# Batches 1 to 7 of attention + SwiGLU: from a planned order to an order written out over ten streams

## The chip, the cores and the metric

The kernel runs on one core of a Trainium2 chip. The metric is device time in microseconds (us), as the median of the runs shown. Five engines work side by side, each through its own queue in order: TensorE (PE in the profile; its weight loads are PEld), VectorE (DVE), ScalarE (ACT), GpSimd (POOL) and SyncE (SP), which issues the DMAs.

## The reference

Two blocks follow each other. First, an attention between the tokens of a sequence and a small set of states, in both directions, for 8 batches and 8 heads (`x` is 8 x 8 x 512 x 64, `state` 8 x 8 x 32 x 64):

```python
scores = scale * np.matmul(x, state.transpose(0, 1, 3, 2))
a = softmax(scores)                     # over the 32 states
xread = np.matmul(a, state)
scores2 = scale * np.matmul(state, x.transpose(0, 1, 3, 2))
a2 = softmax(scores2)                   # over the 512 tokens
sread = np.matmul(a2, x)
attn_out = np.concatenate([xread, sread], axis=2)
```

The result, 8 x (512 + 32) rows of 512 (heads side by side), goes through an RMS norm and a SwiGLU feed-forward with a hidden width of 1536:

```python
xn = x / sqrt(mean(x * x) + 1e-6) * rms_g
g = xn @ w_gate
silu = g * (1.0 / (1.0 + np.exp(-g)))
val = xn @ w_val
out = silu * val @ w_out
```

All is float32; the three weights arrive in float64 and are converted on the chip.

## The kernel before, in words

**Stages.** Weights are converted while batch 0 is computed. Then come batches 1 to 7 (512 token rows each), and last one stage for the 256 state rows of all batches.

**Own weights.** The token read of a batch is a product of softmax weights and 32 states, so the kernel does not form `xn`. It multiplies the states into gate and val weights first (`own_weights`, L430: 16 matmuls on quarters of the array at L437, two copies by ACT to `v` at L446), and the hidden product is then softmax weights times `v`. The raw weights lie in DRAM in six parts `w_m`; `fetch` loads part n + 3 into the buffer that part n leaves (three buffers).

**Products by sevens.** In batches 1 to 7 a product of 2 x 2 blocks is done with seven block products instead of eight. POOL forms the sums of blocks: `slot_sums` (L505) of the softmax weights, four instructions a batch, and `more_of_v` (L457) of `v`, four a pair. `hidden_seven(b, mp)` (L514) does one pair of hidden tiles out of six: seven products of four matmul instructions (L522), into three PSUM banks x, y, z (pool `fx` has two banks, `fy` and `fz` one each). ACT copies x, z, x out (L532, L534, L539), DVE adds y, z, x (L537, L541, L543), ACT does tanh (L547), DVE makes silu x val (L548, L552). From the fourth pair on DVE also makes sums for the projection (L557, L559). `project_seven` (L616) is the projection by `w_out`: seven products of 24 matmul instructions (L626), each in two row halves r, over banks x, y, z again; ACT keeps four results (L646), DVE adds three (L651) and updates the block sums `s` twice (L659, L668); each half of a result is stored by a DMA on SP.

**Attention inside.** In the loop over batches (L743) the attention of batch b + 1 runs beside the products of batch b: `tokens_read` (L251: transposes, scores at L275, softmax on DVE and ACT, the reads at L320, sums of squares at L334, the norm at L344) and `states_read` (L348). `some(n)` advances it by n steps at given places. POOL's `pow` at L238 makes the inverse root.

**What sets the order.** In batch 0 a string, `ORDER` (L22), deals out single steps of fourteen streams under `tc.manual_schedule` (L726), and PE, DVE and ACT keep that order. From batch 1 on nothing is fixed: a planner orders each engine's instructions by what it takes to be ready, by its own costs; the order of the program is only a priority. POOL and SP are the planner's throughout. An instruction that waits holds back all behind it on its engine.

Of the kernel before, what the change touches and what calls it, by code (L numbers as in the profile page):

```python
# [26 lines left out]
    "AhwpuSSSkkkwSwkpSkpwpSSckSScckkpcSwkkk"  # L27
# [4 lines left out]
def kernel(  # L32
# [364 lines left out]
    def attention(b):  # L397

        if 2 < b + 1 < B:
            load_state(b + 1)  # L400
            load_x(b + 1)
        for part in (tokens_read(b), states_read(b)):
            for step in part:
                if step:
                    yield

    def state_norm():

        sq = one.tile([P, NI, NT], F32, name="sqT", tag="eS")
        SE.activation(out=sq, in_=xsT, func=ACTF.Square, scale=DM ** -0.5)  # L410
        sp = aps.tile([P, NT // P], F32, name="at")
        for r in range(NT // P):
            for i in range(NI):
                TE.matmul(out=sp[:, r:r + 1], lhsT=sq[:, i, P * r:P * r + P], rhs=ones,
                          start=(i == 0), stop=(i == NI - 1))
        ss = two.tile([P, NT // P], F32, name="sst")
        VE.tensor_scalar(ss, sp, 1e-6, None, op0=ALU.add)
        rp = along_rows(mean_root(ss, NT // P), NT // P)
# [11 lines left out]
    def own_weights(b, mp):  # L430

        w = w_sb.pop(b * (NM // 2) + mp)
        pv = [vps.tile([P, 4 * P], F32, name="pv") if b else
              aps.tile([P, 4 * P], F32, name="at") for e in range(2)]
        for j in range(4):
            for e in range(2):
                TE.matmul(out=pv[e][Ns * j:Ns * j + Ns, :],  # L437
                          lhsT=stT_g[b][D * e:D * e + D, j, :],
                          rhs=w[D * e:D * e + D, j].rearrange("p m k f -> p (m k f)"),
                          start=True, stop=True)  # L440
# [10 lines left out]
        yield  # L451

    def make_v(b, mp):
        for _ in own_weights(b, mp):
            pass
# [58 lines left out]
    def hidden_seven(b, mp):  # L514

        v, vs = v_sb.pop((b, mp))
        tt = aT_t[b]
        b11, t3, b21, b22 = (aT_s[b][:, e, HS * i:HS * i + HS] for e in range(2) for i in range(2))
# [6 lines left out]
        a11, a12, s3, a22 = (v[:, e, :, k, :] for k in range(2) for e in range(2))  # L525
        g = two.tile([P, 2, 2, HS], F32, name="g", tag="g")
        c22 = seven["c22"].tile([P, 2, HS], F32, name="c22")
        xs = fx.tile([P, 2, HS], F32, name="f")
        ys = fy.tile([P, 2, HS], F32, name="f")
        zs = fz.tile([P, 2, HS], F32, name="f")  # L530
        product(xs, a11, b11, True)
        SE.copy(g[:, :, 0, :], xs)  # L532
        product(zs, vs[:, 0], tt[:, 0], True)
        SE.copy(c22, zs)  # L534
        yield
        product(ys, a12, b21, True)
        VE.tensor_tensor(out=g[:, :, 0, :], in0=g[:, :, 0, :], in1=ys, op=ALU.add)  # L537
        product(xs, vs[:, 1], tt[:, 1], False)
        SE.copy(g[:, :, 1, :], xs)  # L539
        product(zs, vs[:, 2], b22, False)  # L540
        VE.tensor_tensor(out=g[:, :, 1, :], in0=g[:, :, 1, :], in1=zs, op=ALU.add)  # L541
        product(xs, s3, t3, False)
        VE.tensor_tensor(out=c22, in0=c22, in1=xs, op=ALU.add)  # L543
        yield
        h = hb[:, 2 * mp:2 * mp + 2, :]
        gate = g.rearrange("p m c t -> p m (c t)")
        SE.activation(out=h, in_=gate, func=ACTF.Tanh, scale=0.5)  # L547
        VE.scalar_tensor_tensor(out=h, in0=h, scalar=1.0, in1=gate, op0=ALU.add, op1=ALU.mult)  # L548
        product(xs, a22, tt[:, 2], False)
        for i, val in enumerate((xs, c22)):  # L550
            half = h[:, :, HS * i:HS * i + HS]
            VE.scalar_tensor_tensor(out=half, in0=half, scalar=0.5, in1=val,  # L552
                                    op0=ALU.mult, op1=ALU.mult)
        if 2 * mp >= HM:
            k = 2 * mp - HM
            upper, lower = (hb[:, k:k + 2, HS * i:HS * i + HS] for i in range(2))
            VE.tensor_tensor(out=seven["s"][:, k:k + 2, :], in0=lower, in1=h[:, :, HS:S],  # L557
                             op=ALU.add)
            VE.tensor_tensor(out=lower, in0=upper, in1=lower, op=ALU.subtract)  # L559
        yield  # L560
# [37 lines left out]
    def prepare(b):  # L598
        if b < B:
            slot_sums(b)  # L600
            make_v(b, 0)

# [13 lines left out]
    def project_seven(n, store, between, prepare):  # L616
# [4 lines left out]
        def product(ps, lhs, rhs, start):  # L621


            for r in range(R):
                for k in range(HM):
                    TE.matmul(out=ps[:, r, :], lhsT=lhs(k)[:, P * r:P * r + P], rhs=rhs(k),  # L626
                              start=(start and r == 0 and k == 0),
                              stop=(k == HM - 1), skip_group_check=True)

# [12 lines left out]
        def keep(ps):  # L642

            kept = [pool.tile([P, HD], F32, name="ot2") for r in range(R)]
            for r in range(R):
                SE.copy(kept[r], ps[:, r, :])  # L646
            return kept

        def finish(kept, ps, i, j):
            for r in range(R):  # L650
                VE.tensor_tensor(out=kept[r], in0=kept[r], in1=ps[:, r, :], op=ALU.add)  # L651
                store(R * i + r, HD * j, HD, kept[r])

        zs = fz.tile([P, 2, HD], F32, name="f")
        product(zs, S_, TS(0), True)
        p5 = keep(zs)
        for r in range(R):
            c = slice(P * r, P * r + P)
            VE.tensor_tensor(out=s[:, :, c], in0=s[:, :, c], in1=hb[:, 0:HM, c], op=ALU.subtract)  # L659
        xs = fx.tile([P, 2, HD], F32, name="f")  # L660
        product(xs, A(0, 0), B(0, 0), True)
        p1 = keep(xs)
        between()
        product(xs, S_, TS(1), False)
        u2 = keep(xs)
        for r in range(R):
            c = slice(P * r, P * r + P)
            VE.tensor_tensor(out=s[:, :, c], in0=hb[:, HM:NM, c], in1=s[:, :, c], op=ALU.subtract)  # L668
        between()
        product(xs, A(1, 0), B(0, 1), False)  # L670
        finish(p5, xs, 1, 1)
        ys = fy.tile([P, 2, HD], F32, name="f")
        product(ys, A(0, 1), B(1, 0), True)
        finish(p1, ys, 0, 0)
        between()
        prepare()
        product(zs, S_, B(1, 1), False)
        finish(u2, zs, 0, 1)
        product(xs, A(1, 1), TS(2), False)
        for r, c21 in enumerate(keep(xs)):  # L680
            store(R + r, 0, HD, c21)
        between()
# [22 lines left out]
    def first_of_batch_1():  # L705
        slot_sums(1)
        yield
        yield from own_weights(1, 0)
        yield
# [6 lines left out]
    for k in range(1, RAW_AHEAD):  # L716
# [8 lines left out]
               "w": first_of_batch_1(), "k": weight_sums()}  # L725
    with tc.manual_schedule(engines={mybir.EngineType.PE, mybir.EngineType.DVE,  # L726
                                     mybir.EngineType.Activation}):
# [5 lines left out]
    for stream in streams.values():  # L733
        for _ in stream:
            pass
# [3 lines left out]
    def some(n):  # L739
        for _ in range(n):  # L740
            next(steps, done)

    for b in range(1, B):  # L743
        steps = attention(b + 1) if b + 1 < B else state_norm()
        pairs = [hidden_seven(b, mp) for mp in range(NM // 2)]
        next(pairs[0])
        for mp, pair in enumerate(pairs):
            if mp + 1 < len(pairs):
                make_v(b, mp + 1)
            next(pair)  # L750
            if mp + 1 < len(pairs):
                next(pairs[mp + 1])
            next(pair)
            some(2)
        project_seven(S, store_tokens(b), lambda: some(5), lambda: prepare(b + 1))
        for _ in steps:
            pass
# [8 lines left out]
    project_seven(NT, store_states, lambda: None, lambda: None)  # L766
# [30 lines left out]
```

## Time and profile before

| | |
|---|---|
| median of 3 runs | 843.95 us (843.67 to 845.07) |
| the profiled execution | 844.68 us, its span 842.9 us |
| granted TensorE clock, mean | 0.984 |
| busy: PE, PEld | 811.1 us (96%), 591.4 us (70%) |
| busy: DVE, ACT, POOL | 474.3 us (56%), 341.4 us (41%), 164.5 us (20%) |
| the chain that ended last | PE 82%, DVE 14%, issue 2%, ACT 1% |
| one of batches 2 to 6 | 92.86 us |

The span goes from the first instruction to the last. A row of the chain of waits has start, length and what was at work ("PE f L626 x18": 18 matmuls into tile f by line 626). A row of the groups has busy time and the mean of one instruction in ns, then the idle time before them and what ended it. A row of the timeline has start and length in us; idle time and its releaser stand in brackets. A row of windows has, for a stretch, its length, then busy time and count of PE, PEld, DVE, ACT and POOL, the granted clock, the share of the DMA engines and GB/s.

### The profile page before, as it was taken

Reading aid. Unit: us, or ns where it says so; the run is one execution under the profiler, and the core shown is the slowest. Engines: PE = TensorE matmul, PEld = TensorE weight load, DVE = VectorE, ACT = ScalarE, POOL = GpSimd, SP = SyncE. Lnnn points to the kernel's source line nnn. Section 1 sums busy time; section 2 is a strip of 40 time slices with the busy share of each in tenths; the row PEclk is TensorE's granted clock in tenths of the full one; section 3 lists DMA queues with packets and bytes.
Section 4 is the critical chain, followed back from the end, with each engine's and each line's share of the span. In section 5 each row is a group of like instructions: output and inputs, shape, how many; then the busy total and the mean of one; then the engine's idle time right before and its main releaser. Section 6 shows DMA issues by size and latency. Waiting matters only on the chain.

```text
span 842.9 us, 11794 instructions
## 1 busy us (share of the span) xinstructions
PE 811.1 (96%) x4678; PEld 591.4 (70%) x4678; DVE 474.3 (56%) x750; ACT 341.4 (41%) x560; POOL 164.5 (20%) x215
## 2 busy tenths in 40 slices
PE   4699999999999999999999999999999999999997
PEld 3243445768876787768776787668776887788886
DVE  5989986695148723693169614792169515651121
ACT  5888755552055313642155304631255304510110
POOL 0000004231134012421143112311223113400000
PEclk8599999999999999999999999999999999999999
DMA  9788736222233033312342043310322023401211
GB/s 293 240 275 291 259 152 200 104 98 54 88 123 140 4 78 128 145 54 51 101 150 101 4 125 125 105 46 13 138 101 100 2 87 113 150 1 38 113 50 26
DMA packets 61591, 94.09 MB, mean 112 GB/s; under 512 B 38752, under 2 KB 46432, under 8 KB 54624
## 3 DMA queue, kind: packets, MB, share of 16 engines
q1 hardware_dynamic: 59456, 92.81, 32.7%
q8 instruction: 37, 0.61, 0.3%
q10 hardware_dynamic: 2080, 0.52, 0.3%
q14 instruction: 18, 0.15, 0.1%
HBM read 78.12 MB, written 15.20 MB: 111 GB/s over the span
## 4 chain that ended last, share of the span: by engine, by line
PE 82%; DVE 14%; issue 2%; ACT 1%; DMA 0%; SPq 0%; POOL 0%; DVEq 0%
PE f L626 33%; PE f L522 24%; PE f L480 5%; PE f L569 4%; PE pv L437 4%; PE pv L480 4%; PE at L266 2%; DVE g L541 1%; DVE g L537 1%; DVE eS L297 1%; PE at L275 1%; PE at L334 1%; DVE c L543 1%; DVE hb L552 1%; DVE hb L548 1%
## 5 line engine op out<-in xcount | busy, mean ns | idle before, releaser
L522 PE MATMUL f<-aT_s,v 128*128 128x256 f32 x504 | 130.9, 393 | 0.0
L522 PEld LDWEIGHTS f<-aT_s,v 128*128 128x128 f32 x504 | 89.3, 189 | 48.0 <-issue 28.5
L626 PE MATMUL f<-wo,hb 128*128 128x256 f32 x540 | 121.5, 380 | 0.0
L626 PEld LDWEIGHTS f<-wo,hb 128*128 128x128 f32 x540 | 102.0, 190 | 15.5 <-ACT ot L646 1.9
L464 POOL TENSOR_TENSOR vs<-v 128x256 f32<-128x256 f32 x42 | 33.2, 791 | 304.4 <-ACT v L446 304.4
L522 PE MATMUL f<-aT_t,vs 128*128 128x256 f32 x336 | 86.7, 380 | 1.9 <-DVE g L541 1.9
L626 PE MATMUL f<-wt,hs 128*128 128x256 f32 x360 | 86.9, 387 | 0.0
L646 ACT COPY ot<-f 128x256 f32<-128x256 f32 x60 | 19.6, 375 | 163.2 <-PE f L626 163.2
L446 ACT COPY v<-pv 128x512 f32<-128x512 f32 x84 | 46.0, 591 | 92.2 <-PE pv L437 92.2
L626 PEld LDWEIGHTS f<-wt,hs 128*128 128x128 f32 x360 | 65.7, 190 | 15.0 <-issue 4.9
L651 DVE TENSOR_TENSOR ot<-ot,f 128x256 f32<-128x256 f32 x45 | 17.2, 418 | 104.4 <-PE f L626 54.8
L522 PEld LDWEIGHTS f<-aT_t,vs 128*128 128x128 f32 x336 | 63.3, 190 | 13.0 <-POOL v L466 4.2
L537 DVE TENSOR_TENSOR g<-g,f 128x512 f32<-128x512 f32 x42 | 28.6, 680 | 75.0 <-PE f L522 72.8
L547 ACT ACTIVATE hb<-g 128x1024 f32<-128x1024 f32 x42 | 44.4, 1056 | 42.3 <-DVE g L541 42.3
L548 DVE SCALAR_TENSOR_TENSOR hb<-hb,g 128x1024 f32<-128x1024 f32 x42 | 51.4, 1224 | 8.2 <-ACT hb L547 8.2
L437 PE MATMUL pv<-w_m,stT_g 64*32 64x512 f32 x672 | 52.9, 600 | 0.0
L238 POOL TENSOR_TENSOR ri<-ss,mhalf 128x4 f32<-128x4 f32 x8 | 9.1, 1142 | 207.3 <-DVE ss L338 113.4
L522 PE MATMUL f<-aT_t,v 128*128 128x256 f32 x168 | 43.8, 383 | 4.0 <-DVE c L543 4.0
L480 PE MATMUL pv<-aT_s,v 128*128 128x512 f32 x96 | 46.4, 624 | 1.1 <-DVE aT_s L344 1.1
L569 PE MATMUL f<-wo,hb 128*128 128x512 f32 x96 | 44.7, 600 | 0.0
L522 PE MATMUL f<-aT_s,vs 128*128 128x256 f32 x168 | 43.1, 379 | 0.0
L541 DVE TENSOR_TENSOR g<-g,f 128x512 f32<-128x512 f32 x42 | 28.7, 682 | 23.9 <-PE f L522 23.9
(117 smaller groups left out, 1261.9 us busy)
## 6 DMA issues: line engine op xcount, KB each, us to landing
w_m<-w_d SPq DMA_DIRECT2D x48, 1024.0 KB, 4.8
x_b<-in_x_dram SPq DMA_DIRECT2D x30, 256.0 KB, 4.8
out_dram<-ot SPq DMA_DIRECT2D x56, 128.0 KB, 1.8
raw<-in_moe_w_val_dram SPq DMA_DIRECT2D x6, 1024.0 KB, 5.2
raw<-in_moe_w_out_dram SPq DMA_DIRECT2D x6, 1024.0 KB, 7.1
w_d<-w_m SPq DMA_DIRECT2D x6, 1024.0 KB, 4.9
raw<-in_moe_w_gate_dram SPq DMA_DIRECT2D x5, 1024.0 KB, 5.5
raw<-in_moe_w_gate_dram SPq DMA_DIRECT2D x2, 512.0 KB, 4.5
```

The source lines that it names most:

```text
L437: TE.matmul(out=pv[e][Ns * j:Ns * j + Ns, :], lhsT=stT_g[b][D * e:D * e + D, j, :], rhs=w[D * e:D * e + D, j].rearrange("p m k f -> p (m k ...
L446: SE.copy(v[:, e].rearrange("p m k f -> p (m k f)"), pv[e])
L464: GE.tensor_tensor(out=vs[:, 0], in0=a21, in1=a22, op=ALU.add)
L480: TE.matmul(out=to[0][:, 0:n], lhsT=lhs(i, k), rhs=r, start=(i == 0), stop=(i == len(rhs) - 1))
L522: TE.matmul(out=ps[:, i, :], lhsT=lhs[:, i, :], rhs=rhs, start=(start and i == 0), stop=True, skip_group_check=True)
L537: VE.tensor_tensor(out=g[:, :, 0, :], in0=g[:, :, 0, :], in1=ys, op=ALU.add)
L541: VE.tensor_tensor(out=g[:, :, 1, :], in0=g[:, :, 1, :], in1=zs, op=ALU.add)
L547: SE.activation(out=h, in_=gate, func=ACTF.Tanh, scale=0.5)
L548: VE.scalar_tensor_tensor(out=h, in0=h, scalar=1.0, in1=gate, op0=ALU.add, op1=ALU.mult)
L569: TE.matmul(out=banks[r], lhsT=hb[:, m, P * r:P * r + P], rhs=wo[:, m, :], start=(m == 0), stop=(m == NM - 1))
L626: TE.matmul(out=ps[:, r, :], lhsT=lhs(k)[:, P * r:P * r + P], rhs=rhs(k), start=(start and r == 0 and k == 0), stop=(k == HM - 1), skip_gr ...
L646: SE.copy(kept[r], ps[:, r, :])
```

## The change

Batches 1 to 7 get an order for PE, DVE and ACT as batch 0 has one. A new string `PERIOD` deals out the steps of one batch over ten streams: h, t, u (hidden products, ACT's part, DVE's part), p, c, k (the projection's), v (own weights of pairs 2 to 5), a and s (the next batch's attention) and w (the next batch's `slot_sums` and own weights of pairs 0 and 1). The same string serves every batch; letters without a stream are passed over in batch 7, where a is the norm of the states, one step in seven.

`hidden_seven` becomes three generators with a new sequence of products. Within pair m: x by the second sum of weights, z by the third, y, x by s3, then the first two products of pair m + 1 (x by a11, z by the first sum), then the last product of pair m. The first row half of the projection's first product stands before the last product of pair 5. The projection begins with x = A00 B00 and comes to z (by sums), y, x (by sums), x = A10 B01, z = S B11, x = A11 T; before it began with z by sums, and y was fifth. Copies and sums out of a bank are dealt by row halves; the copy of u2's first half comes between the halves of the product by sums into x, and the copy of its second half between the halves of the next. `own_weights` makes four steps (matmuls, two copies, POOL's sums), and own weights of two pairs are made ahead: those of batch 1's pair 1 move into the end of batch 0 (four more letters w in `ORDER`). The state stage calls the same projection in a sequence of 16 steps, and is otherwise as before.

The diff, cut to its core:

```diff
+PERIOD = (
+    "hhtvthhthhuhuuhtuuhthatavhuvtaavauhahauahvtutaauhuhtvvuahhaahthvsuvuhhatatuutuhv"
+    "hvtvshushuhsuhtvhuthtvauhuuuuhvhtsuhuussshtsvhsthauushatutuhhuhpuuuhtsuuupsuapau"
+    "aaakcpkcacsppaaakaaapaccpapakaakcaaaaaapaawkwwwpwkwpkppwkwcwck"
 )
...
         for e in range(2):
             SE.copy(v[:, e].rearrange("p m k f -> p (m k f)"), pv[e])
-            if e == 0:
-                yield
-        if b in aT_t:
+            yield
+        if b:
             more_of_v(b, mp)
-        yield
+            yield
...
+            yield from first(0, pairs[0])
+            for mp, q in enumerate(pairs):
+                if mp:
+                    last(pairs[mp - 1])
+                    yield
+                product(q["x"], q["vs"][:, 1], tt[:, 1], False)
+                yield
+                product(q["z"], q["vs"][:, 2], b22, False)
+                yield
+                q["y"] = fy.tile([P, 2, HS], F32, name="f")
+                product(q["y"], q["a12"], b21, True)
+                yield
+                product(q["x"], q["s3"], t3, False)
+                yield
+                if mp + 1 < len(pairs):
+                    yield from first(mp + 1, pairs[mp + 1])
+            last(pairs[-1])
+            yield
...
+        def sums():
+            for mp, q in enumerate(pairs):
+                h = hb[:, 2 * mp:2 * mp + 2, :]
+                g = q["g"]
+                for to, ps in ((g[:, :, 1, :], "z"), (g[:, :, 0, :], "y"), (q["c"], "x")):
+                    VE.tensor_tensor(out=to, in0=to, in1=q[ps], op=ALU.add)
+                    yield
...
+        def products():
+            yield from product("x", A(0, 0), B(0, 0))
+            yield from product("z", S_, TS(0))
+            yield from product("y", A(0, 1), B(1, 0))
+            yield from product("x", S_, TS(1))
+            yield from product("x", A(1, 0), B(0, 1))
+            yield from product("z", S_, B(1, 1))
+            yield from product("x", A(1, 1), TS(2))
+
+        def copies():
+
+            for what, name in (("p1", "x"), ("p5", "z"), ("u2", "x"), ("c21", "x")):
+                for r in range(R):
+                    to = kept[what, r] = pool.tile([P, HD], F32, name="ot2")
+                    SE.copy(to, banks[name][:, r, :])
...
+        def sums():
+            yield from less(s, s, hb[:, 0:HM])
+            yield from add("p1", "y", 0, 0)
+            yield from less(s, hb[:, HM:NM], s)
+            yield from add("p5", "x", 1, 1)
+            yield from add("u2", "z", 0, 1)
...
     for b in range(1, B):
-        steps = attention(b + 1) if b + 1 < B else state_norm()
-        pairs = [hidden_seven(b, mp) for mp in range(NM // 2)]
...
-        project_seven(S, store_tokens(b), lambda: some(5), lambda: prepare(b + 1))
...
+        if b + 2 < B:
+            load_state(b + 2)
+            load_x(b + 2)
+        h, t, u = hidden_seven(b)
+        p, c, k = project_seven(S, store_tokens(b))
...
+        streams = {"h": h, "t": t, "u": u, "p": p, "c": c, "k": k,
+                   "v": (step for mp in range(2, NM // 2) for step in own_weights(b, mp))}
+        if b + 1 < B:
+            streams.update(a=tokens_read(b + 1), s=states_read(b + 1), w=first_of_batch(b + 1))
+        else:
+            others = paced(state_norm())
+            streams["a"] = others
+        with tc.manual_schedule(**by_hand):
+            for stream in PERIOD:
+                if stream in streams:
+                    next(streams[stream])
...
-    project_seven(NT, store_states, lambda: None, lambda: None)
+    p, c, k = project_seven(NT, store_states)
+    for step in (p, c, p, c, k, p, k, p, c, k, p, k, p, k, p, c):
+        next(step)
```

More of the change, by code (lines that the diff above doesn't have):

```diff
@@ L512, in slot_sums, with hidden_seven @@
         GE.tensor_tensor(out=b12, in0=b22, in1=b12, op=ALU.subtract)
[L514 to L518, printed above, removed]
+    def hidden_seven(b):
+        pairs = [{} for mp in range(NM // 2)]
         def product(ps, lhs, rhs, start):
@@ L523, in product @@
                           stop=True, skip_group_check=True)
[L525 to L559, printed above, removed]
@@ L562, in project_as_ready @@
+        return products(), copies(), sums()
     def project_as_ready(banks):
@@ L655, in project_seven @@
[L655 to L682, printed above, removed]
+        kept = {}
+        def products():
+            yield from product("x", A(0, 0), B(0, 0))
[5 more added lines that the diff above has]
+            yield from product("x", A(1, 1), TS(2))
```

146 lines of the change are left out of this document (93 added, 53 removed).

## The prediction

> **What bounds the kernel now.** I read the busy table first, then the chain of waits, then the windows by batch, and the timeline of TensorE where the chain leaves it.
>
> ```profile
> span 842.9 us, 11794 instructions
> PE 811.1 (96%) x4678; PEld 591.4 (70%) x4678; DVE 474.3 (56%) x750; ACT 341.4 (41%) x560; POOL 164.5 (20%) x215
> ...
> PE 82%; DVE 14%; issue 2%; ACT 1%; DMA 0%; SPq 0%; POOL 0%; DVEq 0%
> ```
>
> TensorE sets the end; no transfer does. But its busy time is made of overlapping records, so 96% doesn't say how much is left. The pitch of the starts does:
>
> ```profile
> 779.09 41.44 PE f L480 x192
> 820.52 18.14 PE f L626 x84
> ...
> 838.69 0.37 ACT ot L646
> ```
>
> At the end of the kernel 192 matmuls of 256 columns take 41.44 us, 0.2158 us each (18.14 / 84 agrees), with no wait among them. That is my unit. Now one batch, number 2, from its first product to that of batch 3 (the chain inside a window, which cuts the last row):
>
> ```profile
> 231.95 1.73 PE f L522 x8
> 233.68 1.02 PE pv L437 x16
> 234.70 6.32 PE f L522 x28
> ...
> 241.13 0.44 PE at L266 x4
> ...
> 287.11 0.79 PE at L334 x8
> ...
> 324.81 1.29 PE f L522 x6
> ```
>
> A batch takes 324.81 - 231.95 = 92.86 us. It has six pairs of 28 product matmuls (gate and val, L522) and 168 of projection (L626): 336 x 0.2158 = 72.5 us. The remaining 20.4 us are the other matmuls, and what is lost between them. The chain leaves TensorE for DVE and ACT from about 259 to 282 us, where the next batch's softmax runs beside pairs 4 to 6. The windows of batch 2, of batch 7, and of the stretch of batch 0 that already has its order by hand:
>
> ```profile
> 231.95:324.81 92.86, 91.68 (x567) 69.94 (x567) 50.24 (x83) 34.54 (x62) 23.16 (x29) 1.00 0.28 92
> ...
> 696.26:779.09 82.83, 82.77 (x435) 65.69 (x435) 39.06 (x57) 24.87 (x42) 14.87 (x21) 1.00 0.21 77
> ...
> 80.00:135.40 55.40, 55.40 (x211) 23.58 (x210) 51.98 (x68) 38.44 (x49) 7.62 (x9) 1.00 0.56 196
> ```
>
> The last row is the best witness for this change: where PE, DVE and ACT each follow a written order, TensorE has no idle time in 55.4 us although DVE is busy for 51.98 of them.
>
> **The change, part by part.** It removes no arithmetic in batches 1 to 7: the same matmuls, copies and sums are issued. What can be gained is lost time alone, so I price a batch without it and compare with 92.86.
>
> (a) The reads of the next batch (L320). Now the planner puts them out as their inputs come, and TensorE waits inside them; in the hand-ordered stretch the same 16 matmuls stand together:
>
> ```profile
> 370.81 1.82 PE L320 MATMUL at<-aT_s,rows 32*64 32x512 f32 x6
> ...
> 373.75 1.13 PE L522 MATMUL f<-aT_t,v 128*128 128x256 f32 x4 [0.67 <-DVE c L543]
> 374.82 1.07 PE L320 MATMUL pv<-aT_s,rows 32*64 32x512 f32 x2
> 375.81 0.91 PE L626 MATMUL f<-wt,hs 128*128 128x256 f32 x3
> ```
> ```profile
> 98.01 0.66 PE L320 MATMUL at<-aT_s,rows 32*64 32x512 f32 x4
> ...
> 99.05 3.70 PE L569 MATMUL f<-wo,hb 128*128 128x512 f32 x8
> ```
>
> From 370.81 to 373.75 and from 374.82 to 375.81 are 3.93 us; together they are 1.04. Gain 2.9, and 0.2 for one change of array shape less. The new list puts them behind y (both halves, 5.2 us) and the first half of x by the sums (2.6), 7.8 us after the first product of sums ends. The last softmax steps on DVE are late there, since in its list they stand behind the addition of y:
>
> ```profile
> L651 DVE TENSOR_TENSOR ot<-ot,f 128x256 f32<-128x256 f32 x45 | 17.2, 418 | 104.4 <-PE f L626 54.8 <-issue 49.6
> ...
> L313 DVE STREAM_TRANSPOSE aT_s<-eS 128x512 f32<-128x512 f32 x16 | 11.3, 704 | 0.1
> ```
>
> 5.2 + 0.42 + some 0.55 for the reciprocal + two of 0.7, and five hand-overs of 0.05 to 0.25, make 8.1: I charge 0.3.
>
> (b) Waits for a PSUM bank inside a pair. The product by s3 goes into the bank that ACT has just copied, with one product between; the new sequence has two between each write, copy and next write:
>
> ```profile
> 345.62 0.59 ACT L539 COPY g<-f 128x512 f32<-128x512 f32 x1 [0.74 <-PE f L522]
> ...
> 346.26 1.38 PEld L522 LDWEIGHTS f<-aT_s,v 128*128 128x128 f32 x7 [0.21 <-ACT g L539]
> ```
> ```profile
> 363.10 1.97 PE L522 MATMUL f<-aT_s,v 128*128 128x256 f32 x8
> 365.39 1.10 PE L522 MATMUL f<-aT_t,vs 128*128 128x256 f32 x4 [0.32 <-DVE g L541]
> ```
>
> The weight load is 0.21 late, and costs the matmul stream 0.08 (28 products take 6.32 instead of 6.04, 0.28 more, of which the change of shape around L437 is 0.2). Six times: 0.5. The second fence is a bank that waits for DVE: 365.39 - 363.10 = 2.29 for eight matmuls (1.73), 0.56 once a batch. With two products between (8 x 0.2158 = 1.73) a copy of 0.59 or a sum of 0.68 and its hand-overs fit. Gain 1.05. What waits next is the sum of val (L543), with two products of cover as well.
>
> (c) The split group of own weights with the scores, and the state reads, now and in the hand-ordered stretch:
>
> ```profile
> 350.35 1.04 PE L437 MATMUL pv<-w_m,stT_g 64*32 64x512 f32 x2
> ...
> 352.97 1.13 PE L522 MATMUL f<-aT_s,v 128*128 128x256 f32 x4
> ```
> ```profile
> 389.57 1.40 PE L381 MATMUL at<-x_b,e2T 128*32 128x64 f32 x64
> 390.90 1.13 PE L626 MATMUL f<-wt,hs 128*128 128x256 f32 x4
> ```
> ```profile
> 135.96 1.10 PE L381 MATMUL at<-x_b,e2T 128*32 128x64 f32 x64
> 136.99 1.13 PE L522 MATMUL f<-aT_s,v 128*128 128x256 f32 x4
> 137.96 0.27 PE L392 MATMUL at<-ident,sr 128*128 128x128 f32 x1
> 138.07 1.88 PE L569 MATMUL f<-wo,hb 128*128 128x512 f32 x4
> ```
>
> 2.62 for two groups of 1.02 and 0.2 for the shapes: 0.4 gained; 1.33 against 1.03: 0.3.
>
> The new batch from the bottom: 72.5 of products; six groups of own weights at 1.02 + 0.2 = 7.3; scores 1.2; reads 1.23 + 0.3; state reads 1.2; sums of squares (0.79 above) 0.9; 30 transposes at 0.11 = 3.3. Sum 87.9, a gain of **4.96 a batch**. From the top, (a) to (c) name 3.1 - 0.3 + 1.05 + 0.7 = 4.55; the other 0.4 are slips of 0.1 in the projection, which I don't trace. Bounds: the sum without the 0.3 and with perfect switches is 87.0; from the other side, at least (a) alone goes, 90.0.
>
> (d) The seam of batches 0 and 1. The fence above shows the first product of batch 1 (136.99) put between L381 and L392 while DVE scales the reads; two lists one after the other can't do that, so 0.95 is lost. One group of own weights (1.22) moves ahead to here. Now from 136.99 to 231.95 are 94.96; then: 0.95 + 0.11 + 1.72 of batch 0's last matmuls + 1.22 + 87.9 = 91.9. Gain 3.06.
>
> (e) Batch 7 has 82.83 now. Its new list: 72.5 + four groups 4.9 + state norm 2.2, and a new loss.
>
> ```profile
> 705.16 1.84 PE L414 MATMUL at<-ones,sqT 128*128 128x1 f32 x16
> 706.94 1.05 PE L437 MATMUL pv<-w_m,stT_g 64*32 64x512 f32 x4
> ```
>
> State norm is 706.94 - 705.16 and two transposes. The copy of u2's first half stands between the two halves of the product into that same bank, and again one product later; in batches 1 to 6 the reads and the sums of squares lie between, in batch 7 nothing. Price: a copy of 0.37 (the last row of the second fence), and on either side of it a hand-over of some 0.2, an estimate: in (b) the weight load starts 0.05 behind the copy's end (345.62 + 0.59 to 346.26) and itself takes time. That is 0.8, twice, 1.6. Sum 81.2, gain 1.6; if halves of a bank don't wait for each other, 3.2.
>
> [...]
>
> (f) At nothing: the state stage (the same 276 matmuls; no wait is seen in them now, and the new order keeps a product of 2.6 us behind each sum); fetches of weights, still three groups ahead, the tightest some 20 us; the loads of x, one batch ahead on SP's queue as now. POOL's four sums of weights for a pair start when the pair two before it has left their buffer:
>
> ```profile
> L467 POOL TENSOR_TENSOR vs<-v,vs 128x256 f32<-128x256 f32 x42 | 37.3, 888 | 0.0
> ```
>
> Four of at most 0.89 make 3.5 us beside a pair of about 8; without that cover each of the four pairs would wait some 2 us.
>
> **Sum.** 3.06 + 5 x 4.96 + 1.6 = 29.5 us. The profiled execution took 844.68 (span 842.9 and 1.8 around it), 0.73 above the median of the three runs, 843.95. So 844.68 - 29.5 = 815.2 on its scale, and 843.95 - 29.5 = **814.5** for the median.
>
> **The rivals.**
>
> 1. *The waits come back.* A list stalls at its head, where the planner slipped something else in. In the profile's favour: DVE's list is full around the hand-over to projection. Against it: the row of 80 to 135 us. If two thirds of what (a) to (c) win return (3 us a batch), 814.5 + 6 x 3 = 832; a third gives 823. Chance 0.16.
>
> 2. *Only TensorE's idle time can go.* The batch window has 92.86 - 91.68 = 1.18 idle, batch 7 0.06: 6 x 1.18 = 7, so 837. Against it: a record of 0.38 in a pitch of 0.2158 covers a slip of 0.1 wholly. Chance 0.04. [...]
>
> 3. *DVE becomes the bound, and it gets slower.* The projection's second product needs all six pairs' sums. Ahead of it DVE has:
>
> ```profile
> L548 DVE SCALAR_TENSOR_TENSOR hb<-hb,g 128x1024 f32<-128x1024 f32 x42 | 51.4, 1224 | 8.2 <-ACT hb L547 8.2
> ...
> L541 DVE TENSOR_TENSOR g<-g,f 128x512 f32<-128x512 f32 x42 | 28.7, 682 | 23.9 <-PE f L522 23.9
> ```
>
> A pair is five instructions of 0.68 and one of 1.22, 4.6 us; the last three pairs have two more each: 32 us, and 5 of attention. TensorE's list up to there is 36.2 (42 products) + 4.9 (own weights) + 2.4 (scores, state reads) + 2.8 (25 transposes) + 5.2 (first product) = 51.5 us, of which DVE can use 46, since its first sum waits for five products and a group. So it is late only if its rows grow by a quarter; from 40% on the loss (37 x 1.4 - 46 = 5.8) eats the 4.96. At 50%, 9.5 a batch: 814.5 + 6 x 9.5 = 872. These rows don't vary with their neighbours now. Chance 0.04; with other losses over 5 us a batch, 0.06 for slower.
>
> 4. *The order isn't kept, or buffers undo it:* the time stays at 844. The order of batch 0 is kept in the trace, but for what follows it. Chance 0.03.
>
> **How the numbers follow.** The forecast (809 to 820) has 0.69, rival 1 0.16, rival 2 0.04, no change 0.03, slower 0.06; 0.02 stay below 809. The range holds the forecast and the milder two thirds of rival 1: 808 (every batch at 87.0, no loss in (e)) to 829. About 0.2% (1.7 us) is what a measurement of this kernel can tell from no change. Faster 0.91, same 0.03, slower 0.06.
>
> **What would show it.** Right: a batch of about 88 us from x of pair 0 to the next; L320 in one block of 16; no weight load waiting for L539's copy; two gaps of 0.7 in batch 7's projection. Wrong: TensorE waiting for DVE at the projection's second product or at L320 (rivals 1, 3), for POOL at the product by the first sum of weights (f), or for a fetch at L437.

## The result, and the profile after

The changed kernel takes **811.83 us** (median of four runs, 811.29 to 812.39) against 844.51 for the kernel before, measured beside it (843.67 to 845.18): a ratio of 0.9614, with a 95% interval from 0.9597 to 0.963. The forecast was 814.5. The profiled execution took 811.35, its span is 809.6. Times below are medians too; one execution of the planned order that took 2690.84 us is left out.

The head of the page of the changed kernel, with the busy time of each engine and the chain of waits by engine:

```profile
span 809.6 us, 11777 instructions
PE 785.6 (97%) x4678; PEld 589.2 (73%) x4678; DVE 483.5 (60%) x750; ACT 337.5 (42%) x560; POOL 156.4 (19%) x215
...
PE 94%; DVE 4%; ACT 1%; issue 0%; DMA 0%; SPq 0%; DVEq 0%
```

The same 4678 matmuls now end 33 us sooner, yet PE's share of the span goes only from 96% to 97%: busy time fell with the span, because it had held the lost time. DVE's part of the chain falls from 14% to 4%. The chain inside a window, batch 2 of the changed kernel, from its first product to that of batch 3:

```profile
227.42 1.73 PE f L517 x8
...
302.27 1.02 PE pv L438 x16
303.29 2.79 PE f L665 x12
...
315.06 1.08 PE f L517 x5
```

A batch is 315.06 - 227.42 = 87.64 us, where it was 92.86, and no row of the window's chain is on another engine than PE. The windows of this batch, of batch 7 and of the state stage up to the start of its last matmul, then two rows of TensorE's waits, summed over the kernel (us in total, times, longest):

```profile
227.42:315.06 87.64, 87.64 (x567) 69.49 (x567) 51.76 (x83) 34.03 (x62) 21.75 (x29) 1.00 0.31 97
665.63:746.75 81.12, 81.12 (x427) 67.70 (x427) 39.34 (x57) 25.74 (x43) 12.35 (x17) 1.00 0.19 65
746.75:804.94 58.19, 57.73 (x267) 50.49 (x267) 11.74 (x29) 5.99 (x16) 0.00 (x0) 1.00 0.19 65
```
```profile
PE at L375 <- ACT e L368: 5.6, 1, 5.6
...
PE f L665 <- ACT ot L698: 0.5, 1, 0.5
```

Everything in that list but the wait at L665 lies ahead of batch 1. The waits of before for the sums (L522 for c L543 and g L541, 4.0 and 1.9 us in all) are gone. Where the 33.3 us of the two profiled spans come from, by the start of the first product matmul of each stage:

| stage | before | after | change | forecast |
|---|---|---|---|---|
| up to batch 1's first product | 136.99 | 136.24 | -0.75 | 0 |
| batch 1 with the seam behind batch 0 | 94.80 | 91.02 | -3.78 | -3.06 |
| batches 2 to 6, each | 92.86 | 87.64 | -5.22 | -4.96 |
| batch 7 and the state stage, to the last matmul | 142.18 | 139.47 | -2.71 | -1.6 |

0.75 + 3.78 + 5 x 5.22 + 2.71 = 33.34. The first row isn't the change's: the kernels below start batch 1 between 135.7 and 137.3 without a cause in their edits (one that moves this product itself apart). In batches 2 to 6 some 2 us are left above the pitch of 0.2155 to 0.2158 us a matmul, counted from the starts of the matmuls (some 7 before; how much exactly depends on what an undisturbed group of small matmuls is taken to cost). They stand at the changes of array shape alone, some 0.09 ahead of a group of small matmuls, 0.09 inside it and 0.10 behind.

The timeline of TensorE where the next batch's state is read, and in batch 7's projection:

```profile
289.17 2.75 PE L665 MATMUL f<-wt,hs 128*128 128x256 f32 x12
291.86 0.66 PE L326 MATMUL at<-aT_s,rows 32*64 32x512 f32 x4
291.88 0.66 PE L326 MATMUL pv<-aT_s,rows 32*64 32x512 f32 x4
292.34 0.61 PE L326 MATMUL at<-aT_s,rows 32*64 32x512 f32 x4
292.36 0.61 PE L326 MATMUL pv<-aT_s,rows 32*64 32x512 f32 x4
292.90 2.86 PE L665 MATMUL f<-wt,hs 128*128 128x256 f32 x12
```
```profile
726.73 1.03 PE L476 MATMUL f<-xsT,w_m 128*128 128x256 f32 x4
727.59 2.75 PE L665 MATMUL f<-wt,hs 128*128 128x256 f32 x12
730.18 2.75 PE L665 MATMUL f<-wo,hb 128*128 128x256 f32 x12
732.77 1.03 PE L476 MATMUL f<-xsT,w_m 128*128 128x256 f32 x4
...
794.07 2.75 PE L665 MATMUL f<-wt,hs 128*128 128x256 f32 x12
797.28 2.86 PE L665 MATMUL f<-wo,hb 128*128 128x256 f32 x12 [0.46 <-ACT ot L698]
```

The reads are one block of 16, 291.86 to 292.90. In batch 7 the planner put eight matmuls of the state stage (L476) into the two places where I had forecast waits. In the state stage itself, where nothing is left to put in, the same wait stands at 797.28.

### The profile page after: what moved, and what is told of

It is laid out like the page before. It is cut to its first block, busy times and chain, and to the rows that moved or that the text cites. A ratio compares the mean times of both kernels' runs of the same rounds, so it can differ in the third digit from the quotient of the medians.

```text
span 809.6 us, 11777 instructions
## 1 busy us (share of the span) xinstructions
PE 785.6 (97%) x4678; PEld 589.2 (73%) x4678; DVE 483.5 (60%) x750; ACT 337.5 (42%) x560; POOL 156.4 (19%) x215
## 4 chain that ended last, share of the span: by engine, by line
PE 94%; DVE 4%; ACT 1%; issue 0%; DMA 0%; SPq 0%; DVEq 0%
PE f L665 34%; PE f L517 32%; PE pv L438 5%; PE f L476 5%; PE f L607 5%; PE pv L476 4%; PE at L272 2%; PE at L326 1%; PE at L281 1%; PE at L340 1%; PE at L387 1%; PE at L438 1%; PE at L375 1%; DVE ex L222 1%; DVE raw L218 1%; PE at L251 1%
## 5 line engine op out<-in xcount | busy, mean ns | idle before, releaser
L665 PE MATMUL f<-wo,hb 128*128 128x256 f32 x540 | 123.4, 380 | 0.5 <-ACT ot L698 0.5
L517 PE MATMUL f<-aT_s,v 128*128 128x256 f32 x504 | 121.0, 381 | 0.0
L665 PEld LDWEIGHTS f<-wo,hb 128*128 128x128 f32 x540 | 102.1, 190 | 14.4 <-ACT ot L698 0.9
L517 PEld LDWEIGHTS f<-aT_s,v 128*128 128x128 f32 x504 | 93.6, 190 | 17.6 <-DVE eS L292 5.0
L698 ACT COPY ot<-f 128x256 f32<-128x256 f32 x60 | 20.2, 373 | 179.4 <-PE f L665 179.4
L517 PE MATMUL f<-aT_t,vs 128*128 128x256 f32 x336 | 89.2, 388 | 0.0
L665 PE MATMUL f<-wt,hs 128*128 128x256 f32 x360 | 82.1, 381 | 0.0
L517 PEld LDWEIGHTS f<-aT_t,vs 128*128 128x128 f32 x336 | 61.1, 190 | 25.9 <-issue 17.6
L665 PEld LDWEIGHTS f<-wt,hs 128*128 128x128 f32 x360 | 67.4, 190 | 13.9 <-ACT ot L698 4.9
L460 POOL TENSOR_TENSOR vs<-v 128x256 f32<-128x256 f32 x42 | 30.7, 730 | 193.7 <-ACT v L447 193.7
L476 PE MATMUL pv<-aT_s,v 128*128 128x512 f32 x96 | 45.9, 619 | 1.1 <-DVE aT_s L350 1.1
L438 PE MATMUL pv<-w_m,stT_g 64*32 64x512 f32 x672 | 46.0, 601 | 0.0
L665 PEld LDWEIGHTS f<-wo,hs 128*128 128x128 f32 x180 | 33.2, 190 | 14.1 <-issue 10.1
```

Source lines behind the costliest of these rows:

```text
L438: TE.matmul(out=pv[e][Ns * j:Ns * j + Ns, :], lhsT=stT_g[b][D * e:D * e + D, j, :], rhs=w[D * e:D * e + D, j].rearrange("p m k f -> p (m k ...
L460: GE.tensor_tensor(out=vs[:, 0], in0=a21, in1=a22, op=ALU.add)
L476: TE.matmul(out=to[0][:, 0:n], lhsT=lhs(i, k), rhs=r, start=(i == 0), stop=(i == len(rhs) - 1))
L517: TE.matmul(out=ps[:, i, :], lhsT=lhs[:, i, :], rhs=rhs, start=(start and i == 0), stop=True, skip_group_check=True)
L665: TE.matmul(out=banks[name][:, r, :], lhsT=lhs(k)[:, P * r:P * r + P], rhs=rhs(k), start=(start and r == 0 and k == 0), stop=(k == HM - 1) ...
L698: SE.copy(to, banks[name][:, r, :])
```

## The experiments

Each is an edit of the changed kernel, but one; the kernel before ran beside them (843.99 to 844.17 us). Batch means from one first product to the next, 87.64 in the changed kernel.

### The order by hand taken out

```
-        with tc.manual_schedule(**by_hand):
+        if True:
```

> The changed kernel, but batches 1 to 7 are left to the planner again: the same streams and the same string, which now is only the order of the program. Theory A, that the gain lies in where the steps stand: the planner follows the program closely as long as nothing seems late, so near 812; the own weights that it splits may cost 0.4 in each of six batches as in the kernel before: 814. Rival, that the gain comes from fixing the order of PE, DVE and ACT: the waits at the reads come back, 3 to 5 us a batch, 832 to 844.

> The changed kernel with the hand-dealt order of batches 1 to 7 taken out: the products keep the new sequence of the program, and the planner orders every engine by its costs and due times, as in the kernel before. A look with a profile at where the 7 us lie by which this order took longer than the one by hand (819.0 against 811.8). Theory: TensorE's own order is almost the same, so the loss is in waits of 1.1 to 1.2 us a batch on vector or scalar results that come later in those engines' planned order. Rival: the loss is in one place, batch 7 or the seam behind batch 0, and batches 2 to 6 take 87.6 as with the order by hand.

818.79 us in the first run (819.0 if the execution left out is counted), ratio 0.9697 [0.9681, 0.9713], between the two expectations; 817.97 in the second, one execution, and the trace is of that one. The window of a batch, and the timeline near that batch's end:

```profile
228.30:317.03 88.73, 88.73 (x568) 69.60 (x566) 50.27 (x83) 33.79 (x62) 21.06 (x29) 1.00 0.29 96
```
```profile
300.14 1.04 PE L438 MATMUL pv<-w_m,stT_g 64*32 64x512 f32 x2
301.11 2.86 PE L665 MATMUL f<-wo,hb 128*128 128x256 f32 x12
...
304.34 1.08 PE L438 MATMUL pv<-w_m,stT_g 64*32 64x512 f32 x14
305.35 2.86 PE L665 MATMUL f<-wo,hs 128*128 128x256 f32 x12
```

A batch takes 88.73, 1.09 more, in each of batches 2 to 6. Both expectations of the second run are wrong. There is no new wait, and it isn't one place: in each of batches 1 to 6 the planner tears two matmuls off a group of own weights. Those two take 301.11 - 300.14 = 0.97, the other fourteen 1.01 (304.34 to 305.35), and a whole group of sixteen 1.02 (302.27 to 303.29 in the changed kernel): in that whole group eight start within 0.05 us of each other (from 302.20) and the next eight 0.45 later (from 302.65), and two torn off in the kernel before also start 0.45 apart (350.35 and 350.80), so two cost as much as sixteen. So 25 to 26 of the 32 us need only the new sequence and the dealt order as the order of the program, left to the planner; the manual order itself is worth 6.1 to 7.0 us (817.97 or 818.79 against 811.83), most of it this one group a batch.

### The order by hand for TensorE alone

```
-        with tc.manual_schedule(**by_hand):
+        with tc.manual_schedule(engines={mybir.EngineType.PE}):
```

> The changed kernel with the written order for PE alone in batches 1 to 7; DVE and ACT are the planner's. Theory A: 812 to 814, since DVE and ACT have time to spare (51.8 and 34.0 us busy in a batch of 87.6). Rival, that the lists of DVE and ACT carry the gain: PE waits for late sums, 820 or more.

811.61 us, 0.9617 [0.9602, 0.9631], a batch of 87.67: no difference. With TensorE's list as dealt, the planner's own order of DVE and ACT serves it as well.

### The reads of the state put early

```
-    "aaakcpkcacsppaaakaaapaccpapakaakcaaaaaapaawkwwwpwkwpkppwkwcwck"
+    "aaakcpkcacsppaaakaaaapccpapakaakcaaaaaapaawkwwwpwkwpkppwkwcwck"
```

The fence shows the second try. The first moved another letter a, some places before this one, which brings two softmax steps forward and no read. TensorE's order stayed as it was, so its 811.63 us (0.9611 [0.9595, 0.9627]) say only that these two steps have room.

> The changed kernel with one letter moved: the reads of the next batch stand one half product earlier on PE, before the product by the sums into x and not between its halves. By step (a), DVE ends the softmax just when the reads start now, so PE waits about 2.6 us in each of six batches, and by step (e) the two halves, no longer apart, wait 0.8 for the copy: 3.4 a batch, 20 us more, 832. Rival, that the place in the list matters little because the inputs are ready: 812, or 817 for the halves alone.

The second moved the right one. This letter holds all the reads, all 16 matmuls, and not only the first as its expectation has it; they now stand ahead of both halves of the product by the sums into x:

> The changed kernel with one letter of its hand-written order moved: in batches 1 to 6 the first of the four reads of the attention's state (L326) stands ahead of projection's product by the sums into x, instead of directly ahead of the other three; every result is the same. Theory (the gain came from reads that no longer stand alone, behind a vector copy that is late): each of the six batches loses again about 2.6 us in front of that first read, and 0.8 where the half copy is waited for; 6 x 3.4 = 20 us, so about 832. Rival (the vector copy is early enough by now, TensorE reaches the read no sooner than its operand): nothing but one more change of array shape, 6 x 0.2, so 812 to 813. Between them, 817, if only the half copy is waited for.

837.9 us, 0.9927 [0.9912, 0.9942]. Timeline of TensorE in batch 2, and windows behind the wait in batches 2 and 6:

```profile
292.77 1.07 PE L326 MATMUL at<-aT_s,rows 32*64 32x512 f32 x2
295.25 0.65 PE L326 MATMUL at<-aT_s,rows 32*64 32x512 f32 x3 [1.41 <-DVE aT_s L319]
...
296.31 4.49 PE L665 MATMUL f<-wt,hs 128*128 128x256 f32 x12
301.25 0.92 PE L665 MATMUL f<-wt,hs 128*128 128x256 f32 x3 [0.46 <-ACT ot L698]
```
```profile
295.25:299.70 4.45, 4.45 (x22) 3.00 (x23) 0.25 (x1) 0.00 (x0) 0.00 (x0) 0.62 0.17 47
665.18:669.60 4.42, 3.96 (x27) 2.49 (x27) 0.74 (x2) 0.48 (x2) 0.00 (x0) 1.00 0.11 33
```

In batches 1 and 6 a batch takes 3.2 us more. 1.57 of that is a gap of 2.00 between two starts in place of 0.43 inside the reads, 0.63 the wait for the half copy and 0.1 its restart, and the rest, 0.9, the block that is torn in two: two of its matmuls run ahead alone. That is about the 3.4 that was expected. In batches 2 to 5 it takes 4.84 more: behind the same wait the clock granted falls to 0.62 of full speed over 4.45 us (batch 2), and matmuls there start 0.43 apart. 2 x 3.2 + 4 x 4.84 = 25.8, of 26.1 measured. So one letter in the wrong place costs 26 us, and 6.6 of them are a cost that neither theory had and that the kernel before doesn't pay (its granted clock is 1.00 in every window from 100 to 820 us).

### y first in each pair

```
-    "hvtvshushuhsuhtv ... tatutuhhuhpuuuhtsuuupsuapau"
+    "hvvshtushuhsuhtv ... tatuuhthuhpuuuhtsuuupsuapau"
...
+                q["y"] = fy.tile([P, 2, HS], F32, name="f")
+                product(q["y"], q["a12"], b21, True)
+                yield
...
-                for to, ps in ((g[:, :, 1, :], "z"), (g[:, :, 0, :], "y"), (q["c"], "x")):
+                for to, ps in ((g[:, :, 0, :], "y"), (g[:, :, 1, :], "z"), (q["c"], "x")):
```

The first version has no change of letters; in two pairs of each batch the second half of gate is then copied ahead of the product by the second sum of weights, so this version leaves one product out of that half.

> The changed kernel with y first in each pair again (y, x by the second sum, z by the third, x by s3), its sum first on DVE; all else as dealt. By step (b): one product less between x's copy and x by s3, so a late weight load in each of 42 pairs, 0.08 us each: 3.4 us more, 815. Rival, that the sequence of the products is of no account since the order is fixed: 812.

821.69 us, 0.9729 [0.9713, 0.9745], a batch of 89.06. Of the 1.42 more, one wait for the copy of x is 1.10. The second version has every copy behind its product:

> The changed kernel with y ahead of z in each pair of batches 1 to 6 (the product by the half-bank copied last comes first), and the two copies of x kept behind their product; every result is the same. Theory (a late weight load costs the product stream 0.08 us where the copy of the same bank stands directly ahead): 42 places x 0.08 = 3.4 us, so about 815. Rival (the copy lies under the products before it): no change, 812.

814.73 us, 0.9654 [0.9638, 0.967]. A batch, and the waits of the weight loads on that copy, which don't occur in the changed kernel:

```profile
227.22:315.26 88.04, 88.04 (x567) 69.21 (x566) 51.58 (x83) 34.29 (x62) 21.71 (x29) 1.00 0.30 97
```
```profile
PEld f L517 <- ACT g L568: 7.7, 36, 0.2
```

0.40 more a batch is five slips of 0.08, seen in the starts of the matmuls (the sixth pair has other work between). In each of these five places a weight load 0.2 late costs 0.08 of the stream.

### The new place of y in the kernel before

```
-        product(ys, a12, b21, True)
-        VE.tensor_tensor(out=g[:, :, 0, :], in0=g[:, :, 0, :], in1=ys, op=ALU.add)
...
         VE.tensor_tensor(out=g[:, :, 1, :], in0=g[:, :, 1, :], in1=zs, op=ALU.add)
+        product(ys, a12, b21, True)
+        VE.tensor_tensor(out=g[:, :, 0, :], in0=g[:, :, 0, :], in1=ys, op=ALU.add)
```

> The kernel before with one edit: y and its sum come after z by the third sum of weights. By step (b) the 42 late loads go (0.08 us each) and with them the wait of 0.56 in each of six batches only if the planner keeps the bank free: 3.4 to 6.7 us less than the kernel before, 838 to 841. Rival, that the planner undoes it or that the time is taken back elsewhere: within 1.5 us of the kernel before.

851.02 us, 1.0079 [1.0064, 1.0094]: slower by 7, a batch of 94.08. One of its waits of TensorE, and DVE's timeline ahead of that wait's end in batch 2:

```profile
PE f L522 <- DVE g L539: 6.4, 6, 1.1
```
```profile
269.81 1.07 DVE L557 TENSOR_TENSOR hs<-hb 128x512 f32<-128x512 f32 x1
270.80 1.21 DVE L311 TENSOR_TENSOR eS<-eS,z 128x512 f32<-128x512 f32 x1
271.94 1.21 DVE L559 TENSOR_TENSOR hb<-hb 128x512 f32<-128x512 f32 x1
273.07 0.68 DVE L539 TENSOR_TENSOR g<-g,f 128x512 f32<-128x512 f32 x1
```

The slip behind the copy is gone (its row counted 42 before, 9.5 us in all). The loss is one place a batch, where the next pair's product into z waits for DVE's sum out of that bank (L539): 1.07 in batch 2, with the restart some 1.3. That bank has more cover than before, three products where it had two. But the sum comes late: three rows of DVE ahead of it take 1.07, 1.21 and 1.21 us here, and 0.67 to 0.69 in the kernel before. That is 1.45 us, more than the wait, in each of batches 1 to 6. What made them grow the run doesn't show. So it doesn't tell what the sequence inside a pair is worth by itself, only that in this kernel it is no gain.

### One list for all batches

```
     with tc.manual_schedule(**by_hand):
-        for stream in ORDER:
+        if True:
+            for stream in ORDER:
...
-        with tc.manual_schedule(**by_hand):
-            for stream in PERIOD:
+            if True:
+                for stream in PERIOD:
...
-    p, c, k = project_seven(NT, store_states)
+        p, c, k = project_seven(NT, store_states)
```

> The changed kernel with one written order from batch 0 to the end of the state stage, not one for each batch, so that the planner has nothing to put between. By step (d) 0.95 us is lost at the seam of batches 0 and 1, and by step (e) 1.6 in batch 7 where eight matmuls of the state stage stood: 2.5 more, 814.4. Rival, that nothing was put in there because of a need: 811.8.

813.03 us, 0.9633 [0.9617, 0.965]. Its waits of TensorE that the changed kernel lacks:

```profile
PE f L665 <- ACT ot L698: 1.4, 3, 0.5
...
PE at L398 <- DVE sr L394: 0.7, 1, 0.7
```

The one list reaches from batch 0 to the end of the state stage, and nothing of a later stage can be slipped in now. Batch 7's projection waits twice, and each time costs 0.63 of wait and 0.10 of restart, 1.46 together. At the seam TensorE waits 0.9 from the end of the state reads to L398, but from the state reads to batch 2 it takes 92.51 against 92.05, so only 0.46 of that is lost. The rest comes back by fewer changes of shape, as I read the two timelines.

### DVE loaded

```
+                for _ in range(2):
+                    VE.reduce_max(out=..., in_=seven["t"][:, 0, 0:4]...)
```

> The changed kernel with two more DVE instructions in each pair, maxima over 1024 columns of a constant tile that nobody reads (about 1.2 us each). By rival 3's count DVE then has 37 + 14.7 = 51.7 us ahead of the projection's second product, and 46 to do them in: 5.7 late in each of six batches, 1 in batch 7, 35 us more, 847. If the slack is larger than that count: 812 to 820.

832.76 us, 0.9863 [0.9848, 0.9878]. A window as long as a batch, and the waits of TensorE (projection's products are L668 here):

```profile
226.00:316.60 90.60, 89.16 (x567) 69.04 (x566) 63.79 (x96) 34.19 (x62) 23.45 (x30) 1.00 0.29 94
```
```profile
PE at L272 <- DVE stT L265: 3.5, 6, 0.8
PE f L517 <- DVE g L579: 2.5, 6, 0.4
...
PE f L668 <- DVE hs L595: 1.5, 6, 0.2
```

DVE has 63.79 - 51.76 = 12.0 us more in a batch, and the batch takes 2.97 more. By my sum for rival 3 (37 us of work, 46 to do it in) 37 + 12.0 - 46 = 3.0. The size agrees, the place doesn't. By the starts of the matmuls, restarts included, only 0.5 of the 2.97 stand at projection's second product, which is where that sum has them; 0.75 are at the transposes of x (L272) and 1.7 at the products of the pairs. So the agreement of the total is in part luck. DVE's slack in this kernel is some 9 us a batch, an estimate from this one load (12.0 - 2.97).

### Groups of one shape put together

Two kernels. In the first the own weights of a pair follow directly behind the scores, in the second the scores stand directly ahead of those of pair 4. Both also make y of the state stage in two halves, so that a product stands between u2's copy and the next one:

```
-    "...tvvuahhaahthvsuvuhhatatuutuhv"
+    "...tvvuavvhhaahthsuuhhatatuutuhv"
...
-    "...tvvuahhaahthvsuvuhhatatuutuhv"
+    "...tvvuhhhthvuavaasuhhatatuutuhv"
...
-    for step in (p, c, p, c, k, p, k, p, c, k, p, k, p, k, p, c):
+    for step in (p, c, p, c, k, p, p, c, p, k, k, p, k, p, k, p, c):
```

> The changed kernel with two edits. Own weights of pair 4 stand right behind the scores, so that the array changes its shape once less in six batches: 0.2 each, 1.2. In the state stage the y product is cut in two, one half on either side of the product by the sums into x, so that the second copy of x is covered: 0.7. Together 1.9 less, 809.9. Rival, that a change of shape costs nothing or the copy of own weights is late for it: 811.5 to 813.

812.43 us, 0.9621 [0.9607, 0.9635]. The state stage no longer waits (0.63 gained), but the own weights moved behind the scores wait for v's copy, 0.4 a batch, which takes back the change of shape (a batch of 87.71), and those of batch 7 wait 0.7.

> The changed kernel with two edits: in batches 1 to 6 the scores stand directly ahead of the own weights of pair 4, so that one change of array shape a batch goes (6 x 0.2 = 1.2 us, if v's copy is not waited for), and in the state stage y is made in two halves so that the product behind u2's copy no longer waits (0.63 us). Theory: 811.8 - 1.8 = 810.0. Rival (moving the scores makes the exponent or the copy of v late by as much): 811.2 to 812.

818.09 us, 0.9689 [0.9674, 0.9703]; a batch of 88.81. Timeline of DVE in batch 2, and of TensorE:

```profile
247.91 0.69 DVE L579 TENSOR_TENSOR g<-g,f 128x512 f32<-128x512 f32 x1 [1.11 <-PE f L517]
250.64 0.72 DVE L292 STREAM_TRANSPOSE eS<-at 128x512 f32<-128x512 f32 x1 [2.04 <-PE at L281]
252.01 0.69 DVE L362 TENSOR_REDUCE m<-sS 128x1 f32<-128x512 f32 x1 [0.65 <-ACT sS L294]
252.62 0.68 DVE L579 TENSOR_TENSOR g<-g,f 128x512 f32<-128x512 f32 x1
...
253.84 0.65 DVE L579 TENSOR_TENSOR c<-c,f 128x512 f32<-128x512 f32 x1
```
```profile
252.31 1.03 PE L517 MATMUL f<-aT_t,vs 128*128 128x256 f32 x4
254.54 1.13 PE L517 MATMUL f<-aT_t,v 128*128 128x256 f32 x4 [1.21 <-DVE c L579]
```

The change of shape is saved, but DVE stands 2.04 and 0.65 us at the head of its list, for scores that come later now, with the sums of the pair behind them, and TensorE then waits 1.21 for the sum of val. 6 x 1.17 - 0.63 = 6.4, of 6.26 measured. The state stage's edit alone, by its 0.63, would give about 811.2; it wasn't run by itself, and the difference is less than a measurement can tell. No run is clearly faster than the changed kernel.

## Why the prediction was right, point by point

The range held the time; the forecast was 2.7 us high. In the two spans that is 33.34 - 29.5 = 3.8, of which 0.75 is the start, 0.72 the seam, 1.30 the five batches and 1.11 the end.

**The unit and what can go.** That only lost time between the matmuls could go, and that TensorE's idle time (rival 2, 837) was no measure of it, is shown: 5.22 a batch went where 1.18 was idle. Batch 2 in both traces, from each matmul's start to the next one's, summed by line (a change of shape counts with the matmul ahead of it):

| step, matmuls | before | after | gain | forecast |
|---|---|---|---|---|
| (a) the reads | 3.94 | 1.04 | 2.9 | 3.1 - 0.3 |
| (b) products of the pairs | 38.39 | 37.35 | 1.04 | 1.05 |
| (c) own weights, scores, state reads | 9.05 | 8.17 | 0.88 | 0.7 |
| all others | 41.50 | 41.08 | 0.41 | 0.4 |

So the steps are right one by one, and not only in sum. The last row wasn't traced in the prediction and was put down to the projection, a guess; 0.35 of it is at the transposes, 0.15 at the projection, and 0.09 went the other way.

**(a) The reads.** Right: one block, no wait. The reads put early again cost 3.2 a batch, of which 0.7 is a wait for the half copy that wasn't there before; 2.5 is the step's own kind of loss. The 0.3 charged for a late DVE was wrong: its last softmax step begins at 290.98 in batch 2 and takes 0.71, so it ends 0.17 ahead of the reads. The load of the reads' weights was 0.3 late, and the stream lost 0.1 at that place, as behind the other changes of shape in batch 2 (0.08 to 0.10). Without the charge the sum is 87.6, which is what was measured.

**(b) The waits for a bank.** Right: the rows for the copy (42 times) and for the sums are gone, and the run with y first gives back 0.08 for each slip. In the kernel before five of the six pairs of batch 2 slip by 0.08, so 0.4 in place of the 0.5. What the step didn't say is that y moved in the kernel before loses 7 us, in a place where three rows of DVE grow.

**(c) Split groups.** Right in size. The planned run shows the mechanism alone: two small matmuls torn off make a batch 1.09 longer.

**(d) The seam.** Here a step failed: "two lists one after the other can't do that, so 0.95 is lost". The planner still moved batch 1's first product (136.24) between the state reads and L398, across the bound of the two lists. In one list TensorE does wait, 0.9, but 0.46 is all that is lost to the planner's way. So the seam gave 3.78, not 3.06: 0.46 more by this, and 0.26 by a batch that was shorter than summed. (The sum's 94.96 runs from a start to a row of the chain, which begins 0.16 behind the matmul; between starts it is 94.80.)

**(e) Batch 7.** The price was right, its effect wrong. The price of 0.8 a place measures 0.73 in the run with one list (0.63 and 0.10), and 0.73 in the state stage. That the halves of a bank wait for each other, on which the choice of 1.6 and not 3.2 rests, was the author's estimate. In the changed kernel ACT's copy of the second half starts at 732.97, only behind the product into the first half (730.18 to 732.94), though its own product stands ahead of that one and ACT had been idle for 5.67 us; in the run with one list TensorE waits three times for ACT's copy (L698, 1.4 in all, 0.5 at the longest). But in the changed kernel the planner filled both places with matmuls of the state stage, again across the bound of a list. I had overlooked that such bounds hold what is inside a list, and not what comes in from the next.

**(f) At nothing.** Right for fetches, loads and POOL. Wrong for the state stage: "keeps a product of 2.6 us behind each sum" is true of the sums, but u2's copy is waited for there as it would be in batch 7, with nothing to fill it: 0.73. So batch 7 and the state stage together gained 2.71: 3.44 in batch 7, where the sum without the price has 3.2, less this wait.

**The rivals.** Rival 1 (waits come back) didn't happen, but the run with the scores moved shows it is real: scores that come later make DVE's list stall, for 1.17 a batch. Rival 3 (DVE as the bound) has its point of decision about where I put it, 9 us more a batch, but the waits spread over three places, and most aren't at projection's second product. Its remark that these rows don't vary with their neighbours holds for the kernel before only (L541 takes 0.67 to 0.69 in all 42 places there, with POOL's sums beside it or without): with y moved three rows grow to 1.07 to 1.21 us, and in the changed kernel one row in each batch (L595) takes 1.16 in place of 0.69, each time with POOL's sums of v beside it (L460 and L461 in batch 2, from 262.46). DVE had the room for it.

## What to carry to other kernels

Price lost time from the starts of the matmuls against their undisturbed pitch, stage by stage, and not from idle time. In an order by hand look first for torn groups of small matmuls and for a step at the head of an engine's list whose input was moved. And where sections written by hand stand next to planned work, don't charge a wait at the bound before looking for what the planner can put into it.

## What the runs showed of the hardware that I had not expected

**The clock after a short wait.** A wait of 1.41 us on TensorE, in the run with the reads put early, was followed in four batches of six by the clock granted at half, for 3.41 us in batch 2 (matmuls 0.43 apart in place of 0.2155). Windows in batch 2, the stretch with the wait and the one at half clock, and two as long in batch 6, the bound between them inside the wait:

```profile
292.82:296.23 3.41, 2.00 (x17) 0.36 (x16) 2.47 (x6) 0.00 (x0) 0.00 (x0) 1.00 0.11 38
296.23:299.64 3.41, 3.41 (x15) 2.71 (x9) 0.00 (x0) 0.00 (x0) 0.00 (x0) 0.50 0.22 61
661.46:664.87 3.41, 2.31 (x9) 0.99 (x7) 1.91 (x5) 0.00 (x0) 0.00 (x0) 1.00 0.11 38
664.87:668.28 3.41, 3.10 (x24) 2.06 (x25) 0.56 (x2) 0.00 (x0) 0.00 (x0) 1.00 0.14 43
```

The wait is the same in both, 3.41 - 2.00 = 1.41 in batch 2 and 1.10 + 0.31 in batch 6, and in batch 6 the clock stays at 1.00, as in batch 1 (1.00 over the 4.40 us behind the wait, from 204.40). In the run with the scores moved it stays at 1.00 over the 88.81 us of batch 2, with a wait of 1.21 in it; in the changed kernel it is 1.00 from 136 to 804 us, where the longest wait is 0.46. So a wait of 1.41 can cost more than itself here, but what decides whether the clock falls behind it these runs don't show.

**Small matmuls.** A group of 2, 14 or 16 matmuls in tiles of 64 x 32 takes 0.97, 1.01 and 1.02 us (the first two in the order by hand taken out, the third in the changed kernel).
